# Attention's output products: sixteen to a step in place of up to eighteen

## The chip, the cores and the metric

The kernel runs on one core of a Trainium2 chip. The metric is the device time of one launch in microseconds (us); less is better. Before the change three runs gave 750.22, 750.38 and 750.85 us.

The engines have the names of the profile: PE is TensorE's matmuls and PEld its weight loads, DVE is VectorE, ACT is ScalarE, POOL is GpSimd, and SP issues most of the DMAs.

## The reference

An attention with a feature map for 8 batches of 8 heads, 576 positions and head width 64, and behind it a layer of experts to which each token goes alone.

```python
proj = x @ w_phi                                  # 64 -> 128, for q and for k
proj = proj - max(abs(proj), axis=-1)
phi = concatenate([exp(proj), exp(-proj)])        # 256 features
kv, z = k_phi.T @ v, k_phi.sum(axis=seq)
out = (q_phi @ kv) / (q_phi @ z + 1e-6)           # the attention's output, x of the next part
...
e = argmax(x @ w_gate), or the expert of the token before, by a local gate
out = softmax(x @ w_gate)[e] * (relu(x @ w1[e]) @ w2[e])    # 8 experts, 512 -> 1024 -> 512
```

## The kernel before

**The work.** Attention is done first, then the experts. Two batches and two heads make a unit, and 16 units make the whole. A unit has 1152 tokens, which are 9 chunks of 128; chunk 4 lies half in the one batch and half in the other. Four units (all heads of two batches) make a quarter of the tokens, called bp in the code.

**The steps.** `run` calls `step(p, n)` for p = 0 to 71, two chunks to a step, and goes on with steps without new chunks (the tail) until all is dealt out. TensorE's instructions stay in the order in which they are written; the order of the other engines' instructions is laid out ahead of time by a scheduler and is fixed in the program as well. A step writes, in this order:

- `proj(p)`, L277: the projections of two chunks, k and q, into a PSUM tile pj, of which there are two. VectorE takes the maximum m of it (L280) and subtracts it (sb, L282), ScalarE makes the k features kp out of sb with two exponentials (L286).
- `qtr(p - 1)`, L295: the transposes of the q part of sb from the step before, into the pj tile of that step. ScalarE makes the q features qp from it (L310). In some steps four more transposes follow, those of a finished sum kvs, and ScalarE copies them out (ks, L374). The projections of the step after need this pj tile, so they wait for the last of these reads.
- the chores: some instructions of the gate, the plan and the experts' first weights, which run beside attention.
- sometimes a gate of a sum: a product with the gate's weights into a PSUM tile nm (L383), which ScalarE adds to kvs (L385). Behind it the output products that use the sum are put into the list `todo`.
- the sums over the keys, kvp, of the chunks of step p - 1 (L327, and L340 for chunk 4). When five chunks are in a sum, ScalarE copies it to kvs (L361, L362).
- output products from the head of `todo` (L405), as many as `QUOTA` allows. A chunk has 8 of them, each of which the profile counts as two matmuls. They go in groups of two or three chunks to one nm tile, of which there are two. With the last product of a group its end is written: VectorE adds, takes the reciprocal and multiplies (rc L422 and L423, xo L425), POOL adds the gate's part to lg (L431 to L434), and SP stores xo (L437).

A unit needs five chunks for its first sum and five for the second, so 72 products of one unit come into the list in two portions, 32 and 40, and with two chunks to a step 4.5 steps go by for a unit. Steps come in five kinds by what they hold beside the projections, the transposes and the sums: the four more transposes (a "ks step"), a gate (a "gate step"), chunk 4 (a "kv4 step"), chunk 4 and a gate, and nothing of it. After nine steps, two units, the pattern repeats. The order on TensorE in any row of nine from p = 5 on is: gate, ks, kv4 and gate, ks, gate, ks, gate, kv4, ks.

**The gate of a quarter.** When the last product of the fourth, eighth and twelfth unit has been dealt out, an entry of the list (`ends`, not a product) starts the token gate of that quarter, which the chores then spread over the steps: small VectorE operations on lg (g_mx L567, and more on tiles named g_), four small transposes or products on TensorE (L588, L600, L615, L628 to L633), one exponential on ScalarE (g_ex L648). The last quarter's gate comes in the tail, beside the first experts' work. After the second quarter a plan for the first experts' slots is made in the same way (p_ tiles), their tokens are gathered, and eight of their weight tiles are split by ScalarE (whi, L961) and POOL (wlo, L964).

**The experts** follow the tail: layers 1 and 2 for slots of up to four times 128 tokens, with lines L1084 to L1086 for the matmuls.

Of the kernel before, what the change touches and what calls it, by code (L numbers as in the profile page):

```python
# [33 lines left out]
WE, WR, WL = 8, 3, 2  # L34
FILL = 6
KVLAG = 1
QUOTA = 18

STEP = "step"

# [15 lines left out]
class Kernel:  # L56
# [428 lines left out]
    def step(self, p, n):  # L485
# [24 lines left out]
        for i in pair:  # L510
            if i % NC != 4:
                self.kv(i)
        for _ in range(min(QUOTA, len(self.todo)) if p < n // 2 else len(self.todo)):
            self.todo.pop(0)()
# [840 lines left out]
```

## Time and profile before

| | us |
|---|---|
| median of three runs | 750.38 |
| the profiled execution, whole | 750.71 |
| its span | 748.9 |
| PE busy in it | 725.5 |
| PEld busy | 629.2 |
| DVE busy | 451.6 |
| ACT busy | 340.8 |
| POOL busy | 180.4 |

The span is the stretch from the first to the last instruction that the profile shows; the whole time has 1.81 us more. In the views that follow, times are us from the span's start. A row of a timeline is: start, duration, engine, line, operation, output and inputs, shapes, the number of instructions that the row merges, and in brackets how long the engine was idle before it and which engine's result ended the wait. A row of a table by stretches is: start and end, length, and for each of PE, PEld, DVE, ACT and POOL the busy time with the number of instructions, then the granted clock, the share of the DMA engines and GB/s. In a row of waits stand the total, the number of times and the longest. A busy PE is not PE at its peak: matmuls are pipelined and their ends are modelled.

Attention takes the stretch to about 291 us of the span and the experts the rest.

### The profile page before, as it was taken

To read this page: it belongs to the slowest core of one execution; us is meant where nothing else is said; L and a number is where in the kernel's file an instruction comes from. 1 tells how busy PE (TensorE), PEld (TensorE's weight loads), DVE (VectorE), ACT (ScalarE), POOL (GpSimd) and SP (SyncE) were. 2 spreads that over 40 slices of the span, in tenths; PEclk is the share of its full clock that TensorE was granted. 3 is DMA by queue.
4 is the path that set the end of the run, shared out by engine and by line. 5 is a ranking of instruction groups with operands and counts; after the bars stand their busy time and mean duration, and the time that the engine had idled before them with its cause. 6 is when DMAs were issued, how large, how long until landed. Compare 5 with 4: busy or idle time off the path is not lost. (4 is left out here: it accounts for less than half of the span.)

```text
span 748.9 us, 22153 instructions
## 1 busy us (share of the span) xinstructions
PE 725.5 (97%) x9447; PEld 629.2 (84%) x9447; DVE 451.6 (60%) x828; ACT 340.8 (46%) x644; POOL 180.4 (24%) x306
## 2 busy tenths in 40 slices
PE   6999999999998899999999999999999999999996
PEld 6999989989887888889888975889888778888995
DVE  5888889888878886594536335435522365444413
ACT  5766666666676574323434225332312255241301
POOL 0210103410364674353402041021302102101011
PEclk9999999999999999999999999999999999999999
DMA  7755545554666651064918866334686355434110
GB/s 213 242 169 141 151 129 148 136 157 127 189 191 201 202 176 55 7 198 132 329 63 325 313 237 230 118 127 168 226 291 239 113 221 169 140 127 155 58 39 30
DMA packets 66101, 125.05 MB, mean 167 GB/s; under 512 B 7220, under 2 KB 45300, under 8 KB 65950
## 3 DMA queue, kind: packets, MB, share of 16 engines
q1 hardware_dynamic: 57808, 101.03, 42.1%
q0 software_dynamic: 8016, 22.51, 8.5%
q8 instruction: 75, 1.23, 0.7%
q14 instruction: 26, 0.21, 0.1%
q10 hardware_dynamic: 176, 0.07, 0.0%
HBM read 102.05 MB, written 22.06 MB: 166 GB/s over the span
## 5 line engine op out<-in xcount | busy, mean ns | idle before, releaser
L1129 ACT ACTIVATE hh<-l 128x384 fp32r<-128x384 f32 (+1 forms) x84 | 45.1, 537 | 206.0 <-PE l L1086 206.0
L1084 PE MATMUL l<-xhi,whi 128*128 128x384 f32 (+2 forms) x352 | 124.1, 353 | 0.0
L1086 PE MATMUL l<-xhi,wlo 128*128 128x384 f32 (+2 forms) x352 | 123.6, 351 | 0.0
L1085 PE MATMUL l<-xlo,whi 128*128 128x384 f32 (+2 forms) x352 | 123.3, 350 | 0.0
L1130 DVE SCALAR_TENSOR_TENSOR hl<-l,hh 128x384 fp32r<-128x384 f32 (+1 forms) x84 | 51.6, 615 | 115.9 <-ACT hh L1129 115.8
L1084 PE MATMUL l<-whi,hh 128*128 128x512 f32 x288 | 115.5, 401 | 0.6 <-DVE y L1183 0.6
L964 DVE TENSOR_TENSOR wlo<-wraw,whi 128x1024 fp32r<-128x1024 f32 x80 | 96.5, 1223 | 29.1 <-ACT whi L961 28.9
L1085 PE MATMUL l<-wlo,hh 128*128 128x512 f32 x288 | 113.8, 395 | 0.0
L1086 PE MATMUL l<-whi,hl 128*128 128x512 f32 x288 | 113.7, 395 | 0.0
L286 ACT ACTIVATE kp<-sb 128x512 f32<-128x512 f32 x144 | 83.5, 625 | 59.3 <-DVE sb L282 56.6
L280 DVE TENSOR_REDUCE m<-pj 128x8 f32<-128x1024 f32 x72 | 87.8, 1220 | 35.3 <-PE pj L277 33.3
L961 ACT CAST whi<-wraw 128x1024 fp32r<-128x1024 f32 x88 | 90.4, 1045 | 38.3 <-PE l L1086 14.9
L277 PE MATMUL pj<-first,kq 64*128 64x128 f32 x1152 | 85.2, 289 | 8.3 <-DMA kq<-in_kqT 4.2
L310 ACT ACTIVATE qp<-pj 128x512 f32<-128x512 f32 x144 | 79.7, 595 | 23.5 <-PE pj L295 11.3
L282 DVE TENSOR_TENSOR sb<-pj,m 128x1024 f32<-128x1024 f32 x72 | 88.1, 1223 | 3.5
L405 PE MATMUL nm<-kvs,qp 128*64 128x74 f32 x2304 | 87.2, 228 | 1.9 <-ACT kvs L385 1.0
L277 PEld LDWEIGHTS pj<-first,kq 64*128 64x128 f32 x1152 | 71.5, 191 | 15.4 <-ACT ks L374 5.4
L405 PEld LDWEIGHTS nm<-kvs,qp 128*64 128x64 f32 x2304 | 79.8, 136 | 2.6 <-ACT kvs L385 1.4
L327 PE MATMUL kvp<-v,kp 128*64 128x65 f32 x2048 | 77.7, 225 | 0.8 <-ACT kp L286 0.2
L1186 POOL DMA_INDIRECT out<-y,p_tokm x30 | 34.2, 1141 | 182.4 <-DVE y L1183 165.7
L1084 PEld LDWEIGHTS l<-xhi,whi 128*128 128x128 f32 x352 | 66.2, 188 | 7.2 <-issue 1.6
L327 PEld LDWEIGHTS kvp<-v,kp 128*64 128x64 f32 x2048 | 67.1, 137 | 5.4 <-ACT kp L286 2.0
(224 smaller groups left out, 907.1 us busy)
## 6 DMA issues: line engine op xcount, KB each, us to landing
wraw<-in_w1h SPq DMA_DIRECT2D x44, 512.0 KB, 3.6
wraw<-in_w2h SPq DMA_DIRECT2D x44, 512.0 KB, 5.9
kq<-in_kqT SPq DMA_DIRECT2D x47, 384.0 KB, 4.4
v<-in_va SPq DMA_DIRECT2D x48, 195.0 KB, 3.7
xs<-xo SPq DMA_DIRECT2D x48, 128.0 KB, 2.1
whi<-in_w1h SPq DMA_DIRECT2D x8, 512.0 KB
wlo<-in_w1h SPq DMA_DIRECT2D x8, 512.0 KB, 8.0
whi<-in_w2h SPq DMA_DIRECT2D x8, 512.0 KB
```

The lines of the kernel that those rows point to most:

```text
L277: self.last_pe = self.pe.matmul(t[:, h, i % 2, j, :], kq[r, j, s], self.w2[r], start=True, stop=True)
L280: dve.tensor_reduce(m, f, AX.X, ALU.max, apply_absolute_value=True)
L282: self.last_dve = dve.tensor_sub(sb.rearrange("p h c j f -> p (h c j) f"), f, m.unsqueeze(2).broadcast_to([128, 8, 128]))
L286: self.last_act = act.activation(kp[:, :, :, sg, :].rearrange("p c h f -> p h c f"), sb[:, :, :, 0], AF.Exp, scale=1.0 - 2 * sg)
L310: self.act.activation(qp[:, sg].rearrange("p h (c r k) -> p (h c) r k", c=2, r=2), src, AF.Exp, scale=1.0 - 2 * sg)
L327: self.pe.matmul(t[r, sg, h], kp[:, h, sg, r], v[:, h], start=first and sg + h == 0, stop=last and sg + h == 2)
L405: self.last_num = self.pe.matmul(e["t"][r, c - c0, k], self.ch[i]["qp"][:, sg, h, q0 + r.start:q0 + r.stop], kvs[:, sg, k], start=sg == 0, ...
L961: self.act.copy(hi, raw)
L964: (low or self.dve).tensor_sub(lo[:, c], raw[:, c], hi.bitcast(F32)[:, c])
L1084: mm(o, ah, bh, start=first, stop=False)
L1085: mm(o, ah, bl, start=False, stop=False)
L1086: self.last_pe = mm(o, al, bh, start=False, stop=last)
```

## The change

One constant. `QUOTA` is the most that a step takes from the list of output products, 18 before and 16 now.

```diff
-QUOTA = 18
+QUOTA = 16
```

It is used in the last lines of `step` alone, and not in the tail, where the whole list is dealt out:

```python
for _ in range(min(QUOTA, len(self.todo)) if p < n // 2 else len(self.todo)):
    self.todo.pop(0)()
```

Nothing is added or taken away: the same products are dealt out in the same order, at other places between TensorE's other work, and what depends on a group's last product moves along. Before, nine steps dealt out 18, 14, 18, 18, 18, 18, 18, 18 and 4, which is 144; with the change each deals out 16, 144 as well. The entry that starts a quarter's gate takes a place in the list, so three steps have 15, and from each of them on the list is behind by one more. At p = 72, in the tail, 43 products are left in place of 36.

The first place is on TensorE, in the steps p = 12 to 14, a kv4 step, a ks step and a gate step. The rows are instructions in their order, and the number behind x says how many stand together. Before:

```order
L405 MATMUL nm<-kvs,qp 64x74 x18
L277 MATMUL pj<-first,kq 128x128 x8
L295 MATMUL pj<-first,sb 128x64 x8
L295 MATMUL pj<-first,kvs 128x64 x4
L327 MATMUL kvp<-v,kp 64x65 x16
L405 MATMUL nm<-kvs,qp 64x74 x4
L277 MATMUL pj<-first,kq 128x128 x8
L295 MATMUL pj<-first,sb 128x64 x8
L383 MATMUL nm<-wgi,ks 64x18 x4
L327 MATMUL kvp<-v,kp 64x65 x16
L405 MATMUL nm<-kvs,qp 64x74 x18
```

And now:

```order
L405 MATMUL nm<-kvs,qp 64x74 x16
L277 MATMUL pj<-first,kq 128x128 x8
L295 MATMUL pj<-first,sb 128x64 x8
L295 MATMUL pj<-first,kvs 128x64 x4
L327 MATMUL kvp<-v,kp 64x65 x16
L405 MATMUL nm<-kvs,qp 64x74 x16
L277 MATMUL pj<-first,kq 128x128 x8
L295 MATMUL pj<-first,sb 128x64 x8
L383 MATMUL nm<-wgi,ks 64x18 x4
L327 MATMUL kvp<-v,kp 64x65 x16
L405 MATMUL nm<-kvs,qp 64x74 x16
```

The ks step in the middle had 4 products and has 16; its neighbours have two fewer each.

The second place is on VectorE, where the first quarter's gate begins: the m and sb in these rows are those of p = 23, g_ are the gate's tiles, and the xo ahead is that of the quarter's last group. Before:

```order
L425 TENSOR_TENSOR xo<-nm,rc 128x296
L567 TENSOR_REDUCE g_mx<-lg 128x9
L577 SCALAR_TENSOR_TENSOR g_rs<-lg,consts 128x9
L570 TENSOR_TENSOR g_eq<-lg,g_mx 128x72
L280 TENSOR_REDUCE m<-pj 128x8
L572 TENSOR_TENSOR g_eq<-g_eq,consts 128x72
L282 TENSOR_TENSOR sb<-pj,m 128x1024
L574 TENSOR_REDUCE g_fr<-g_eq 128x9
L646 TENSOR_TENSOR g_ls<-lg,g_mx 128x72
L580 TENSOR_TENSOR g_code<-consts,g_fr 128x9
L581 TENSOR_TENSOR g_code<-g_code,g_rs 128x9
L422 TENSOR_SCALAR rc<-nm 128x4
```

And now:

```order
L425 TENSOR_TENSOR xo<-nm,rc 128x296
L567 TENSOR_REDUCE g_mx<-lg 128x9
L577 SCALAR_TENSOR_TENSOR g_rs<-lg,consts 128x9
L570 TENSOR_TENSOR g_eq<-lg,g_mx 128x72
L646 TENSOR_TENSOR g_ls<-lg,g_mx 128x72
L572 TENSOR_TENSOR g_eq<-g_eq,consts 128x72
L280 TENSOR_REDUCE m<-pj 128x8
L574 TENSOR_REDUCE g_fr<-g_eq 128x9
L282 TENSOR_TENSOR sb<-pj,m 128x1024
L580 TENSOR_TENSOR g_code<-consts,g_fr 128x9
L651 TENSOR_REDUCE g_su<-g_ex 128x9
L581 TENSOR_TENSOR g_code<-g_code,g_rs 128x9
```

Five of the gate's operations stand ahead of the m where three stood, and no rc and xo stand between the m of p = 23 and that of p = 24; before, those of a group of the next unit stood there. For the second and the third quarter the gate's first operations stand one step later than before, in p = 41 in place of 40 and in p = 59 in place of 58, and seven and nine of them are ahead of the m that follows.

## The prediction

> **What bounds the kernel now.** I read the page first, then a table by stretches of the span, cut at the starts of nine-step patterns (units in pairs) and at the experts:
>
> ```profile
> span 748.9 us, 22153 instructions
> ...
> 53.12:86.50 33.38, 33.28 (x873) 31.63 (x873) 29.10 (x55) 23.13 (x52) 3.64 (x16) 1.00 0.53 146
> 86.50:122.61 36.11, 35.12 (x887) 32.25 (x887) 31.72 (x75) 22.90 (x53) 2.91 (x13) 1.00 0.47 134
> 122.61:155.93 33.32, 33.22 (x873) 31.57 (x873) 27.93 (x43) 23.24 (x52) 14.05 (x33) 1.00 0.54 148
> 155.93:192.04 36.11, 35.18 (x886) 32.25 (x886) 31.72 (x75) 22.89 (x53) 3.04 (x14) 1.00 0.48 135
> 192.04:228.86 36.82, 34.28 (x874) 31.79 (x874) 30.12 (x62) 25.88 (x55) 20.57 (x43) 1.00 0.67 206
> 228.86:269.16 40.30, 35.74 (x888) 32.71 (x888) 33.46 (x77) 26.65 (x57) 22.32 (x43) 1.00 0.62 192
> ...
> 300.00:741.00 441.00, 440.37 (x2384) 364.75 (x2382) 205.68 (x341) 145.33 (x210) 87.82 (x81) 1.00 0.49 171
> ```
>
> The experts' stretch is TensorE's without a break: 440.37 of 441 us. So what attention gains or loses moves the end by as much. In attention the six rows hold the same 72 steps' kind of work, 144 products each, and yet take from 33.3 to 40.3 us. The first and third row are clean. The second, fourth and sixth hold a quarter's gate, the fifth the plan and the first weight tiles. Weight loads take 31.6 us of a clean nine and 32.7 of the worst, so the excess is waiting, mostly. Who TensorE's queue waits for, from p = 5 to 67, its three largest rows:
>
> ```profile
> PEld pj L277 <- ACT ks L374: 5.2, 13, 1.2
> PEld pj L295 <- DVE sb L282: 3.6, 7, 1.0
> PEld kvp L340 <- ACT kp L286: 2.1, 8, 0.3
> ```
>
> None of it is for products. TensorE waits for what VectorE and ScalarE make of the projections; the products are filler in which these two catch up. The change deals the filler out evenly.
>
> **The steady pattern.** The starts of TensorE's steps, each the row of its projections, p = 6 to 10 and p = 13 to 15:
>
> ```profile
> 23.98 1.16 PE L277 MATMUL pj<-first,kq 64*128 64x128 f32 x16
> 27.42 1.16 PE L277 MATMUL pj<-first,kq 64*128 64x128 f32 x16
> 31.39 1.16 PE L277 MATMUL pj<-first,kq 64*128 64x128 f32 x16
> 35.09 1.16 PE L277 MATMUL pj<-first,kq 64*128 64x128 f32 x16
> 38.90 1.16 PE L277 MATMUL pj<-first,kq 64*128 64x128 f32 x16
> ...
> 50.14 1.16 PE L277 MATMUL pj<-first,kq 64*128 64x128 f32 x16
> 53.12 1.16 PE L277 MATMUL pj<-first,kq 64*128 64x128 f32 x16
> 57.08 1.16 PE L277 MATMUL pj<-first,kq 64*128 64x128 f32 x16
> ```
>
> Differences of neighbours give lengths: a ks step 3.44 us with 14 products and 3.70 with 18, so a product costs 0.26/4 = 0.065 us. A gate step of 18 takes 3.81, one with chunk 4 as well 3.97. The ks step with 4 products should take 3.70 - 14 x 0.065 = 2.79 and takes 2.98, and the gate step behind it 3.96 in place of 3.81. The rows at the end of another such step, p = 22, show why:
>
> ```profile
> 85.97 0.43 PE L405 MATMUL nm<-kvs,qp 128*64 128x74 f32 x8
> 86.06 0.38 ACT L374 COPY ks<-pj 128x256 f32<-128x256 f32 x1
> 86.50 0.97 PEld L277 LDWEIGHTS pj<-first,kq 64*128 64x128 f32 x16 [0.25 <-ACT ks L374]
> ```
>
> The products are through and the next projections wait for ScalarE's ks, which frees their tile. Then sb and kp come late for the step behind. With 16 products the ks step lasts 3.70 - 0.13 = 3.57, and ks is ready 0.6 us before it is wanted. Per nine steps: seven steps lose 2 products (-0.91), one gains 2 (+0.13), the short one goes from 2.98 to 3.57 (+0.59), and the step behind loses its delay (-0.15): -0.34. There are seven short steps (p = 13, 22, ..., 67): **-2.4 us**. Every group's end (rc, xo) still comes once a step; 7 products more in the tail cost 0.45 and are those that steps p = 23 to 71 didn't do, so they cancel.
>
> The Trainium skill (Perfetto Trace Analysis, Identifying the Most-Contended Engine) says that TensorE's headroom is to be judged by its weight loads and not by its matmul rows. In the first clean row the matmuls leave 0.10 us free and the loads 1.75; by the former seven such nines could gain 0.7 us at most, by the latter 12, and my 2.4 lies between.
>
> **The gates of the first two quarters.** The chain at p = 23:
>
> ```profile
> 87.14 0.15 DVE L422 TENSOR_SCALAR rc<-nm 128x4 f32<-128x4 f32 x1
> 87.25 1.15 ACT L286 ACTIVATE kp<-sb 128x512 f32<-128x512 f32 x2 [0.81 <-DVE sb L282]
> 87.49 0.41 PE L295 MATMUL pj<-first,sb 64*128 64x64 f32 x8
> 87.59 0.47 DVE L425 TENSOR_TENSOR xo<-nm,rc 128x296 f32<-128x296 f32 x1
> 88.44 0.22 POOL L434 TENSOR_TENSOR lg<-lg,xo 128x18 f32<-128x18 f32 x1
> 88.70 0.23 DVE L567 TENSOR_REDUCE g_mx<-lg 128x9 f32<-128x72 f32 x1 [0.64 <-POOL lg L434]
> 89.11 1.22 DVE L280 TENSOR_REDUCE m<-pj 128x8 f32<-128x1024 f32 x1
> 90.43 1.23 DVE L282 TENSOR_TENSOR sb<-pj,m 128x1024 f32<-128x1024 f32 x1
> 90.47 1.16 PE L277 MATMUL pj<-first,kq 64*128 64x128 f32 x16
> 94.64 1.16 PE L277 MATMUL pj<-first,kq 64*128 64x128 f32 x16
> 99.69 1.16 PE L277 MATMUL pj<-first,kq 64*128 64x128 f32 x16
> ```
>
> m stands in VectorE's queue behind g_mx, which waits for POOL, which waited for xo. So it starts 2.61 us after its step's start (86.50), where the projections are there after 1.2. The delay reaches TensorE one step later (4.17 for a 14-product ks step of 3.44), and since rc, xo and eight small operations stand ahead of the next m, once more: 5.05 for 3.97. Lost: 0.73 + 1.08 = 1.81, and as much at the second quarter, whose row above has the same 36.11.
>
> With the change, from a step's start at 0 and these rows' distances. First quarter: the last group ends with p = 22, xo is done at 1.0, POOL at 1.55, five small operations take it to 2.3: m is 1.1 late, sb is done at 4.9. The transposes want it at 3.62 + 1.0 and are 0.3 late, the sums want kp, 0.6 later. No xo stands ahead of the next m, so the delay isn't handed on. But the 15 products of p = 23 follow their gate at once and ScalarE has g_ex, which now comes earlier, ahead of what they wait for: I take 0.75 in all. Second quarter: m of p = 41 is ahead of the gate, that of p = 42 starts at 6.2 where 4.8 would do; sb is done at 8.7, wanted at 8.2, and with kp 0.95 is lost, once. **-1.06 and -0.86, together -1.9.**
>
> **What is given back.** Between a gate's start and its end four steps hold its products, and there ScalarE's exponentials wait for VectorE's small operations, not TensorE for its work. Two products fewer don't shorten such a step; the first sum took 0.13 off each. Bounds: nothing, and 4 x 0.13 = 0.52 a gate. I take the upper one, as the rows of waits name ScalarE: 3 x 0.5 = **+1.5**.
>
> **The plan and the third gate.** Steps p = 52, and p = 60 to 62:
>
> ```profile
> 199.48 1.16 PE L277 MATMUL pj<-first,kq 64*128 64x128 f32 x16
> 204.84 1.16 PE L277 MATMUL pj<-first,kq 64*128 64x128 f32 x16
> ...
> 232.67 1.16 PE L277 MATMUL pj<-first,kq 64*128 64x128 f32 x16
> 237.48 1.16 PE L277 MATMUL pj<-first,kq 64*128 64x128 f32 x16 [0.51 <-ACT ks L374]
> 243.01 1.16 PE L277 MATMUL pj<-first,kq 64*128 64x128 f32 x16
> 249.25 1.16 PE L277 MATMUL pj<-first,kq 64*128 64x128 f32 x16 [1.03 <-ACT ks L374]
> ```
>
> Step p = 52 loses 5.36 - 3.97 = 1.39 to the plan's block of small operations ahead of m. The block moves one step on, behind it comes a longer step (3.84 for 3.44), which hides 0.4 of it: bounds 0 and -1.0, I take **-0.5**. The third gate loses 4.81 - 3.44 and 5.53 - 3.97, 2.93 in all. After, as the second quarter's, 0.95, and 0.35 more for two more small operations ahead of m: -1.6. Against it step p = 62 (6.24), where the list's tokens and the gate's code meet, becomes a gate step, in which ScalarE's order puts qp behind the next kp: +0.5. Together **-1.1**; bounds 0 and -2.
>
> **The sum.** -2.4 - 1.9 + 1.5 - 0.5 - 1.1 = -4.4 us: a span of 744.5, and 746.3 for the profiled execution of 750.71. The three runs' median is 0.33 lower, so I put **746.0** against 750.38.
>
> **The rivals.**
>
> *The waits only move* (17%). They belong to the gate and the plan, not to the products, so each is found again a step later. For it: the gate's chain through POOL is the same. Against it: what stands behind that chain has changed. Then only the short steps' -2.4 and the +1.5 are left: 749.5, no change.
>
> *The gaps close* (15%). With even steps the small delays of clean steps vanish as well. Best lengths with 16: four ks steps of 3.57, three gate steps of 3.68, 3.84 and 3.60 make 32.76 a nine, 0.25 under what I counted, seven times; and nothing is given back: 742.7.
>
> *VectorE has no free step* (13%). The place is p = 24 to 29 and the same steps of the other two gates. Before, two steps there (p = 25 and 29) had no xo, and VectorE caught up; with the change each of the six has one. m to sb takes 1.32, sb to rc 1.15, rc to the end of xo 0.92: 3.4 us, and five small operations of up to 0.2 make 4.4. It decides if this exceeds the step, 3.7 to 3.9: 0.45 a step in three steps is 1.35 a gate and 4.0 in all, in the place of the +1.5. With the short steps' -2.4 and no other gain that is +1.6, **752.0**. Against it: VectorE's 31.72 of 36.11 leaves over 4 us a nine.
>
> That the change deals otherwise than it says is ruled out by the order, but for three steps of 15.
>
> **Chances and range.** The forecast has 55% (744 to 748.5). A measurement can tell about 0.2%, 1.5 us, from no change. Faster: the forecast, the closed gaps and a little of the moved waits, 0.73; within 0.2%: 0.15; slower: 0.12. The range, 742.9 to 750.6, takes in the unknown costs' bounds and the moved waits, and leaves out the free-step rival and half of the closed gaps.
>
> **What would show it.** Right: every ks step at 3.57 and none near 2.98; no wait of L277 for ks in clean nines, which take 33.0; the nines with the first two gates at 35.2 and 35.4, that of the third near 39.4; the experts' stretch as before, shifted. Wrong: xo ending later than the next step's projections step after step, or nines with gates at 36 or more.

## The result, and the profile after

The changed kernel took 747.65 us in the median, beside 751.57 for the kernel before in the same comparison; the ratio is 0.9944, with a 95% interval of 0.9933 to 0.9955. Two later comparisons, on two chips, gave 0.9925 (0.9906 to 0.9944) and 0.9910 (0.9895 to 0.9925). One run of the change (992.03 us, mean granted clock 0.667) and one of the kernel with QUOTA = 32 further down (794.51 us, 0.885) stand apart and are in none of the ratios. It is faster by 4 to 7 us; 746.0 was forecast against 750.38, a ratio of 0.9942.

The profiled execution took 747.42 us. Its span, from the page:

```profile
span 745.6 us, 22169 instructions
```

The stretches, cut at the same steps as before (p = 14, 23, 32, 41, 50, 59 and 68, and 441 us of the experts):

```profile
53.91:86.96 33.05, 33.05 (x877) 31.49 (x873) 29.38 (x55) 23.31 (x52) 3.67 (x16) 1.00 0.54 149
86.96:121.91 34.95, 34.12 (x887) 32.08 (x884) 31.02 (x71) 23.02 (x53) 2.26 (x10) 1.00 0.50 142
121.91:154.80 32.89, 32.87 (x876) 31.35 (x873) 28.04 (x44) 23.39 (x52) 14.01 (x34) 1.00 0.54 149
154.80:190.48 35.68, 34.70 (x888) 32.23 (x885) 31.70 (x74) 23.05 (x53) 3.06 (x13) 1.00 0.48 137
190.48:225.03 34.55, 33.63 (x876) 31.57 (x873) 29.77 (x63) 24.86 (x54) 19.37 (x42) 1.00 0.67 201
225.03:265.08 40.05, 35.68 (x890) 32.75 (x886) 33.65 (x76) 27.26 (x58) 21.55 (x42) 1.00 0.67 203
...
296.00:737.00 441.00, 439.89 (x2382) 364.35 (x2381) 205.49 (x341) 145.29 (x210) 89.51 (x82) 1.00 0.49 171
```

A row of nine steps is called a nine from here on. Every nine is shorter than before. The fifth row, with the plan, lost 2.3 us, the second, with the first gate, 1.2, and the sixth, with the third gate, a quarter. In the experts PE is busy throughout, as before. TensorE's queue, over the same steps, waits much less for ks, sb and kp, and in the second place stands a wait that was not among its largest:

```profile
PEld pj L277 <- ACT ks L374: 2.6, 7, 0.5
PEld nm L405 <- ACT kvs L385: 1.5, 3, 0.7
PEld pj L295 <- DVE sb L282: 1.3, 3, 0.7
```

The steps p = 12 to 14, each row the start of a step's projections:

```profile
46.73 1.16 PE L277 MATMUL pj<-first,kq 64*128 64x128 f32 x16
50.34 1.16 PE L277 MATMUL pj<-first,kq 64*128 64x128 f32 x16
53.91 1.16 PE L277 MATMUL pj<-first,kq 64*128 64x128 f32 x16
57.59 1.16 PE L277 MATMUL pj<-first,kq 64*128 64x128 f32 x16
```

The ks step p = 13 takes 3.57 where it took 2.98, the gate step behind it 3.68 where it took 3.96. The chain of the first gate, from p = 23 on:

```profile
86.96 1.16 PE L277 MATMUL pj<-first,kq 64*128 64x128 f32 x16
89.32 0.26 ACT L648 ACTIVATE g_ex<-g_ls 128x72 f32<-128x72 f32 x1 [1.06 <-DVE g_ls L646]
89.35 1.22 DVE L280 TENSOR_REDUCE m<-pj 128x8 f32<-128x1024 f32 x1
90.21 1.24 PE L405 MATMUL nm<-kvs,qp 128*64 128x74 f32 x30 [0.53 <-ACT kvs L385]
91.38 1.16 PE L277 MATMUL pj<-first,kq 64*128 64x128 f32 x16
92.59 1.23 DVE L280 TENSOR_REDUCE m<-pj 128x8 f32<-128x1024 f32 x1
95.01 1.16 PE L277 MATMUL pj<-first,kq 64*128 64x128 f32 x16
98.85 1.16 PE L277 MATMUL pj<-first,kq 64*128 64x128 f32 x16
```

p = 23 to 25 take 4.42, 3.63 and 3.84, where they took 3.97, 4.17 and 5.05. The delay is taken once, by the products of p = 23, which wait for kvs behind g_ex. The m of p = 24 starts 1.21 after its step's start. Before, it started 3.16 after it (90.47):

```profile
93.63 1.16 DVE L280 TENSOR_REDUCE m<-pj 128x8 f32<-128x1024 f32 x1
```

The third gate has kept two long steps. In p = 61, which takes 5.87, the cause lies one step earlier, in p = 60, which starts at 229.09: its m stands behind the gate's first nine operations on VectorE, g_mx among them, which waits 1.17 for POOL's lg. So it starts 3.04 after its step:

```profile
232.13 1.22 DVE L280 TENSOR_REDUCE m<-pj 128x8 f32<-128x1024 f32 x1
```

The other is p = 63, with waits as large as those of p = 62 before:

```profile
242.48 1.16 PE L277 MATMUL pj<-first,kq 64*128 64x128 f32 x16
243.76 1.23 DVE L280 TENSOR_REDUCE m<-pj 128x8 f32<-128x1024 f32 x1 [0.21 <-PE pj L277]
243.81 0.38 PE L754 MATMUL pj<-first,lr 6*128 6x6 f32 x2
244.97 0.15 DVE L757 COPY p_probe<-pj 128x6 f32<-128x6 f32 x1
245.18 0.28 PE L588 MATMUL pj<-first,g_code 128*9 128x128 f32 x1 [0.98 <-DVE p_probe L757]
...
248.81 1.16 PE L277 MATMUL pj<-first,kq 64*128 64x128 f32 x16 [1.01 <-ACT qp L310]
```

The list's tokens are transposed (L754), their copies stand behind m on VectorE, and the gate's next operation on TensorE waits for the copies; the step takes 6.33, where p = 62 took 6.24.

### The profile page after: what moved, and what is told of

Same layout as the page of the kernel before. It is cut to its first block, busy times and chain, and to the rows that moved or that the text cites. A ratio compares the mean times of both kernels' runs of the same rounds, so it can differ in the third digit from the quotient of the medians.

```text
span 745.6 us, 22169 instructions
## 1 busy us (share of the span) xinstructions
PE 724.3 (97%) x9447; PEld 630.2 (85%) x9447; DVE 451.9 (61%) x828; ACT 341.3 (46%) x644; POOL 182.8 (25%) x305
## 3 DMA queue, kind: packets, MB, share of 16 engines
q8 instruction: 75, 1.23, 0.7%
## 5 line engine op out<-in xcount | busy, mean ns | idle before, releaser
L277 PE MATMUL pj<-first,kq 64*128 64x128 f32 x1152 | 85.8, 290 | 7.5 <-DMA kq<-in_kqT 4.2
L277 PEld LDWEIGHTS pj<-first,kq 64*128 64x128 f32 x1152 | 72.0, 192 | 14.2 <-issue 4.2
L1086 PEld LDWEIGHTS l<-xhi,wlo 128*128 128x128 f32 x352 | 66.2, 188 | 5.5
```

Of the source, the lines that this page charges most:

```text
L277: self.last_pe = self.pe.matmul(t[:, h, i % 2, j, :], kq[r, j, s], self.w2[r], start=True, stop=True)
L1086: self.last_pe = mm(o, al, bh, start=False, stop=last)
```

## The experiments

There were twelve runs, four to a call, those of one call on the same chip; three of them repeat the kernel before or the change. This table of the nines' lengths (us, by the starts of L277) is read with all of them; the last column runs from p = 5 to p = 68.

| first step | 5 | 14 | 23 | 32 | 41 | 50 | 59 | sum |
|---|---|---|---|---|---|---|---|---|
| what is in it | | | gate 1 | | gate 2 | plan | gate 3 | |
| before | 33.17 | 33.38 | 36.11 | 33.32 | 36.11 | 36.82 | 40.30 | 249.21 |
| before, third call | 33.17 | 33.23 | 36.12 | 33.64 | 36.12 | 36.59 | 42.31 | 251.18 |
| the change | 33.03 | 33.05 | 34.95 | 32.89 | 35.68 | 34.55 | 40.05 | 244.20 |
| the change, first call | 33.02 | 33.03 | 34.95 | 32.88 | 35.43 | 34.38 | 40.02 | 243.71 |
| the change, third call | 33.03 | 33.09 | 34.95 | 32.94 | 35.44 | 35.78 | 39.93 | 245.16 |
| short step split | 33.08 | 33.40 | 35.34 | 33.17 | 35.23 | 36.08 | 38.91 | 245.21 |
| QUOTA = 17 | 33.49 | 33.57 | 35.50 | 33.31 | 35.87 | 34.94 | 39.43 | 246.11 |
| gates a step later | 32.95 | 33.17 | 36.15 | 33.11 | 36.28 | 36.61 | 40.46 | 248.73 |
| order alone | 33.69 | 33.17 | 35.40 | 33.53 | 36.72 | 35.88 | 38.97 | 247.36 |
| order alone, third call | 33.18 | 33.50 | 35.41 | 33.58 | 36.74 | 34.84 | 39.49 | 246.74 |
| 16, gates not later | 32.80 | 32.79 | 35.24 | 33.20 | 36.00 | 34.98 | 39.28 | 244.29 |
| QUOTA = 32 | 35.06 | 36.31 | 38.72 | 37.20 | 38.89 | 38.57 | 42.26 | 267.01 |
| 16, tokens a step later | 32.99 | 32.79 | 34.95 | 32.91 | 35.43 | 36.54 | 41.61 | 247.22 |
| 16 and the order | 33.03 | 32.83 | 35.08 | 32.81 | 35.55 | 35.49 | 37.98 | 242.77 |

The first two gates' nines repeat within 0.3 us from execution to execution. The nine with the plan doesn't, for the change 34.4 to 35.8, nor does the third gate's in the kernel before, 40.3 and 42.3. What follows p = 68 takes between 479.0 and 485.0 us of the span in these profiles, for the change alone 479.9 to 483.3. So differences between the whole times of two profiles can't be put down to the edits; the nines and the medians of several runs can.

**The change again**, the code of the change.

> The change once more, beside the three kernels that follow, so that all four stand against the same runs of before. By the first comparison of it, 4.2 us under before (ratio 0.9944).

Measured: 745.88 us against 751.82, ratio 0.9925.

**The short step alone.**

```diff
+        quota = 10 if p % 9 == 3 else QUOTA        # QUOTA stays 18
-        for _ in range(min(QUOTA, len(self.todo)) if p < n // 2 else len(self.todo)):
+        for _ in range(min(quota, len(self.todo)) if p < n // 2 else len(self.todo)):
```

> QUOTA stays at 18, only the step ahead of each short one gives up 8 of its products to it: of nine steps the last two deal 10 and 12 in place of 18 and 4, all others and the steps in which the gates begin stay as before. My theory (products are cover, and the short step has too few of them) gives the short ks step 3.70 - 6 x 0.065 = 3.31 in place of 2.98, the kv4 step ahead of it 8 x 0.065 = 0.52 less, the step behind 0.15 less: -0.34 a nine, seven times, 2.4 us under before (ratio 0.9968), with the gates' nines losing their 1.8 as before. The rival that the gain of the change is all in where the gates begin gives no change (ratio 1.000). The rival that every step must have 16 (the closed gaps) gives less than 1 us.

Measured: 0.9950 (0.9936 to 0.9964), 3.8 us. Neither the sum nor the rival holds. The clean nines gained 0.1 instead of 0.34, and the gates' nines, which were to stay, became shorter by 0.8, 0.9 and 1.4 us. First, why the clean ones gained so little. The starts of p = 12 to 14, and below them the m of p = 12 and 13 on VectorE:

```profile
46.29 1.16 PE L277 MATMUL pj<-first,kq 64*128 64x128 f32 x16
49.52 1.16 PE L277 MATMUL pj<-first,kq 64*128 64x128 f32 x16
52.91 1.16 PE L277 MATMUL pj<-first,kq 64*128 64x128 f32 x16
```

```profile
47.50 1.23 DVE L280 TENSOR_REDUCE m<-pj 128x8 f32<-128x1024 f32 x1 [0.69 <-PE pj L277]
51.10 1.21 DVE L280 TENSOR_REDUCE m<-pj 128x8 f32<-128x1024 f32 x1
```

The two steps take 3.23 and 3.39, together 6.62 where 3.73 + 2.98 = 6.71 stood. VectorE's work from one m to the next takes 3.60 there (m, sb, two small operations on a table, a group's rc and xo), more than either step: the second m starts 1.58 after its step, the first 1.21. The ks step was to take 3.31 and takes 3.39, and p = 14 behind it takes 3.90 where 3.81 was to come. By these rows, what the short step gains in cover its neighbour lacks.

**QUOTA = 17.**

```diff
-QUOTA = 18
+QUOTA = 17
```

> QUOTA = 17: nine steps deal 17, 15, six times 17, and 10, and the gates of the quarters begin in the same steps as with 18. My theory: seven steps with a product less, -0.46, one with one more, +0.07, the short one 3.70 - 8 x 0.065 = 3.18 in place of 2.98, +0.20, the one behind -0.15: -0.34 a nine again, 2.4 us under before; of that up to 0.8 is given back in the gates' steps that are bound by ScalarE: -1.6 to -2.4 (ratio 0.9968 to 0.9979). That the gates' place is the whole: no change. That only the fully even deal helps: less than 1 us.

Measured: 0.9950 (0.9933 to 0.9967). The clean nines got longer, by 0.32 and 0.19 in the first two, where 0.34 was to be gained; what was gained lies in the gates' nines (0.61, 0.24 and 0.87) and in the plan's (1.88). Why a product less in each step gained nothing, the starts of p = 10 to 12 and the weight loads of p = 10's products show:

```profile
39.04 1.16 PE L277 MATMUL pj<-first,kq 64*128 64x128 f32 x16
42.74 1.16 PE L277 MATMUL pj<-first,kq 64*128 64x128 f32 x16
46.54 1.16 PE L277 MATMUL pj<-first,kq 64*128 64x128 f32 x16
```

```profile
41.42 1.23 PEld L405 LDWEIGHTS nm<-kvs,qp 128*64 128x64 f32 x34
```

The ks step with 17 takes 3.70 and the gate step 3.80: as long as with 18. The rows of the same step before, with 18, and in the change, with 16:

```profile
41.29 1.23 PEld L405 LDWEIGHTS nm<-kvs,qp 128*64 128x64 f32 x36
...
41.87 1.10 PEld L405 LDWEIGHTS nm<-kvs,qp 128*64 128x64 f32 x32
```

17 and 18 products take 1.23, 16 take 1.10. Likewise p = 6 takes 3.57 with 15 and with 16. Products cost 0.13 a pair, and an odd one as much as a pair: neighbours in the list go to the two halves of the output's partitions. The Trainium skill (TensorEngine Tiling (Array Packing), Key Properties) says that different tiles of the array can load and multiply in parallel; the trace agrees, the 17th and 18th product go in the time of one.

**The gates a step later.**

```diff
         lt = self.lg.pop(bp)
         if not self.tail:
+            yield STEP
             yield STEP
         L = lt[:, :, 0:E]
```

> QUOTA stays at 18, the gates of the first three quarters wait one step more before their first operation, nothing else is changed. In the first gate's chain g_mx then finds lg long done: the 0.64 of waiting and the chain over xo and POOL go, and five small operations of together 0.9 stay ahead of the m of p = 24. My theory: two thirds of the 1.8 us that each of three gates loses, with the later place of the plan: 2 to 3 us under before (ratio 0.996 to 0.9973), about as much as the gates' terms of the sum without what is given back. The rival that the waits only move: no change (within 0.5 us). The rival of the free step: slower, since p = 24's own xo and the gate's operations meet, by up to 1 us a gate.

Measured: 0.9967 (0.9957 to 0.9977), 2.5 us, as my theory had it, but not by its way. The edit writes all of a gate's operations a step later. Those on TensorE moved (L588 of the first gate from p = 26 to p = 27); VectorE's first ones the scheduler laid out where they had been, among p = 23's:

```profile
89.58 0.23 DVE L568 TENSOR_REDUCE g_mx<-lg 128x9 f32<-128x72 f32 x1 [0.64 <-POOL lg L434]
```

g_mx waits its 0.64 as before, p = 24 and 25 take 4.18 and 5.06 as before, and the nines of the first two gates lose nothing. What moved is the plan: p = 51 and 52 take 7.91 where they took 8.80. In the profiled execution the nines lose 0.5 and what follows them up to the experts 0.9, and the start gives 1.3 back, where the granted clock was 0.57 over p = 2 (3.96 for 2.58). As a test of the gates' place it failed.

**The order alone.** In the change, with 17 and with the split step, all with 10 products or more in p = 22, the gate's g_ls stands ahead of the m of p = 23 on VectorE; in the kernel before it stands behind sb. So this kernel deals as before and only writes g_ls and g_ex earlier.

```diff
         dve.tensor_tensor(eq, L, bc(mx, E), ALU.is_ge)
+        ls = sm([128, NC, E], "ls")
+        with self.soon():
+            dve.tensor_sub(ls, L, bc(mx, E))
+        ex = sm([128, NC, E], "ex")
+        with self.soon():
+            act.activation(ex, ls, AF.Exp)
         yield
...
-        ls = sm([128, NC, E], "ls")
-        dve.tensor_sub(ls, L, bc(mx, E))
-        ex = sm([128, NC, E], "ex")
-        act.activation(ex, ls, AF.Exp)
-        yield
```

> QUOTA stays at 18 and every step deals what it dealt before. Only the gate's subtraction g_ls and its exponential g_ex are written right behind g_eq, and ahead of what isn't the gate's, so that on VectorE and ScalarE the gate's operations stand as they do with 17 and with the split short step: g_ls ahead of the m of p = 23, g_ex ahead of p = 23's qp, and between the m of p = 23 and that of p = 24 three fewer of the gate's operations. Theory of the order (formed from the first four runs: with 17, and with 12 products in the short step, the gates' nines shrank by 0.2 to 0.9 though no gate began later, since the delay is then taken once, at the products of p = 23, and not handed on to p = 25): p = 23 takes about 4.9, p = 24 3.5 and p = 25 4.2, the three gates' nines lose 0.6 to 1.4 each, and the whole is 2 to 3 us under before (ratio 0.996 to 0.9973). My first theory (the products must stand in the short step, and the list must be a step later): the gates' nines stay within 0.2, no change (ratio 1.000).

> The kernel with the old deal and the other order of the gate once more: it came out at 0.9906, lower than the change in either comparison, though on another chip. Theory of the order: it reaches at least half of the change's gain without moving a product, 0.990 to 0.997. If its first result belonged to that chip: 1.000.

Measured: 0.9906 (0.9889 to 0.9923), and in the third call 0.9917 (0.9902 to 0.9933), beside 0.9910 for the change. Without moving a product it reaches the change's time. The steps p = 23 to 25 of the third call, and VectorE's rows among them:

```profile
86.50 1.16 PE L277 MATMUL pj<-first,kq 64*128 64x128 f32 x16
90.12 1.38 PE L405 MATMUL nm<-kvs,qp 128*64 128x74 f32 x36 [0.74 <-ACT kvs L385]
91.43 1.16 PE L277 MATMUL pj<-first,kq 64*128 64x128 f32 x16
94.87 1.16 PE L277 MATMUL pj<-first,kq 64*128 64x128 f32 x16
98.99 1.16 PE L277 MATMUL pj<-first,kq 64*128 64x128 f32 x16
```

```profile
88.97 0.23 DVE L573 TENSOR_TENSOR g_ls<-lg,g_mx 128x72 f32<-128x72 f32 x1
89.12 1.22 DVE L280 TENSOR_REDUCE m<-pj 128x8 f32<-128x1024 f32 x1
92.88 1.21 DVE L280 TENSOR_REDUCE m<-pj 128x8 f32<-128x1024 f32 x1
```

4.93, 3.44 and 4.12: 12.49 where 13.19 stood. A group's rc and xo still stand ahead of the m of p = 24, which starts 1.45 after its step and not 3.16. The theory of the order holds for gates 1 and 3 (-0.7 and -0.8 to -1.3 against the first profile); the nine of gate 2 is 0.6 longer. The edit also takes a yield out of the gate, and the plan behind it now reaches p = 49 (3.94 in place of 2.97), where ScalarE's qp waits 1.32 for the plan's p_ue. So it isn't the whole: by the traces it is worth 1.9 to 2.5 us up to p = 68 against the first profile of before, and 4.4 against that of the third call, where the change has 6.0. That the medians are level (750.66 us beside 750.31) comes from elsewhere: behind p = 68 the third call's profile of the order takes 480.7 us, the change's 483.3 and that of before 484.8. No run shows whether this comes from the edit or from chance.

**Sixteen, with the gates in their old steps.**

```diff
-QUOTA = 18
+QUOTA = 16
...
-                self.todo.append(lambda: self.ends(u // NHP))
+                end = self.todo.pop()
+                self.todo.append(lambda: (end(), self.ends(u // NHP)))
```

> QUOTA = 16, but the entry that starts a gate takes no place of its own in the list: no step has 15, the list isn't put behind, and the gates begin in p = 22, 40 and 58 as with 18, one step earlier than in the change. My term for the gates rests on their place: without it the second gate's nine loses its 0.86 again and the third its 1.6, less 0.5: slower than the change by about 2 us (ratio 0.997 to before). Theory of the order: the even deal alone gives the good order, so the first and second gates' nines are near 35.3 and the third's, without the meeting of the list's tokens and the gate's code behind a gate step, near 39.2: as fast as the change or up to 1.5 us faster (ratio 0.991 to 0.994).

Measured: 0.9936 (0.9922 to 0.9950); a direct comparison with the change on that chip wasn't made. The profiled execution met two falls of the granted clock to 0.50, at 11 to 15 and 328 to 333 us, outside the nines. A clean nine and the first gate's:

```profile
54.04:86.83 32.79, 32.79 (x875) 31.32 (x872) 29.38 (x55) 23.32 (x52) 3.66 (x16) 1.00 0.53 148
86.83:122.07 35.24, 34.29 (x890) 32.18 (x887) 31.43 (x75) 23.03 (x53) 3.14 (x14) 1.00 0.50 138
```

The seven nines sum to 244.29, the change's to 244.20. Beginning a step later, the change gains 0.3 at each of the first two gates and gives 0.8 back at the third: nothing in all. My first theory is out.

**The opposite dose.**

```diff
-QUOTA = 18
+QUOTA = 32
```

> The opposite dose: QUOTA = 32 deals 32, 0, 32, 8, 32, 0, 32, 8, 0 in nine steps, the same 144 products. If the products are cover: a step of 32 takes 3.81 + 14 x 0.065 = 4.72, a ks step of none can't be shorter than the 2.98 of the step with 4 in before, which VectorE's and ScalarE's work sets; four of the former, three of the latter, two with 8 (3.05 and 3.08) and the delays behind make 34.1 to 35 a nine in place of 33.3: 5 to 12 us slower than before (ratio 1.007 to 1.016). If only the gates' order and place counted: within 2 us of before.

Measured: 1.0212 (1.0197 to 1.0228), 16 us slower, above the range given; the nines say the same, +17.8 us in their sum. Two falls of the granted clock are in that sum (0.79 and 0.86 over 90 to 95 and 95 to 100 us, 0.66 over 245 to 250); by one minus the clock, times the stretch, they are worth about 3.4 us, an estimate. The first nine has none:

```profile
19.90:54.96 35.06, 33.92 (x872) 31.73 (x873) 28.69 (x47) 22.78 (x52) 7.05 (x22) 1.00 0.66 203
```

The weight loads hardly changed (31.73, before 31.38): the same products cost the same, and most of the rest is waiting. That products are cover, and that clumps of them are lost cover, holds.

**The tokens a step later**, with QUOTA = 16:

```diff
-WAIT, HOLD = 3, 2
+WAIT, HOLD = 4, 2
```

> The change with one number more: the list's tokens are transposed one step later (WAIT 4 in place of 3), so that they don't fall into the step of the third gate's code, where the step p = 63 takes 6.33 us with 0.98 of waiting for p_probe. If that meeting is the cause, p = 63 falls to about 4, another step gets 0.3 to 0.8 more, and the whole is 1 to 2 us under the change (ratio 0.990 to 0.992 to before). If the wait belongs to the tokens' gather alone (they come late whatever stands beside), the next step gets it: as the change.

Measured: 0.9958 (0.9944 to 0.9971), slower than the change was in the other calls. p = 63 fell to 4.14, and p = 64 took 7.57:

```profile
251.04 0.20 PE L600 MATMUL pj<-g_dg,consts 9*9 9x9 f32 x2 [1.18 <-DVE p_probe L757]
255.59 1.65 PE L277 MATMUL pj<-first,kq 64*128 64x128 f32 x16 [1.95 <-ACT ks L374]
```

The copies stand behind m in this step too, and the gate's next operation on TensorE, now another, waits for them. Meeting the code (L588) wasn't the cause.

**Before, the change, the order and both, on one chip.**

> The kernel before once more, with a profile of its own beside the three that follow. The same code: ratio 1.000. It shows which of the steps that the change seemed to shorten are long in every execution and which only in the first profile: the gates' steps (p = 24 and 25: 4.17 and 5.05; p = 52: 5.36; p = 61 and 62) should be the same within 0.1, while those with an idle time that is put down to issue (p = 53 with 4.73, p = 56 with 4.54) may not. If p = 53 and 56 come out near 3.8, up to 1.8 us of the fifth nine's gain of 2.3 isn't the change's.

> The change a third time, beside its rivals on the same chip: 0.993 to 0.995 of before.

> The change and the order together. The even deal gives the first gate's order by itself already, so nothing is gained there; the clean nines gain their 0.3 (2 us in seven), and in the second and third gates g_ls stands a place or two earlier and the m of p = 59 ahead of the gate's block. If the two gains are of different places: 1 to 2 us under the better of the two (0.988 to 0.992). If they are one and the same: as the change (0.993 to 0.995).

The first three are kernels told of above. The last joins the change to the edit of the order:

```diff
-QUOTA = 18
+QUOTA = 16
...
+        with self.soon():
+            dve.tensor_sub(ls, L, bc(mx, E))
```

Measured: before 0.9999 (757.81 us), the change 0.9910, both together 0.9876 (0.9858 to 0.9893; 748.13 us beside 750.31 for the change). It is the fastest of all, by 0.3% against the change. Its nine with the third gate takes 37.98, where the change has 39.93: p = 61 to 63 take 3.84, 4.07 and 5.35 in place of 5.86, 3.57 and 6.34. In the first two gates nothing is added, as expected: the change has the order there already. In the second profile of before the first two gates' steps repeat (p = 24, 25 and 43: 4.19, 5.05, 5.05). Two others that were expected to repeat don't: p = 52, with the plan, took 5.57 in place of 5.36, and p = 61, in the third gate, 6.93 in place of 5.53. Of the steps with unexplained idle time p = 53 took 3.95 in place of 4.73 and p = 57 4.61 in place of 3.73. So the change's gain in the fifth nine, 2.27 by the first pair of profiles, is 0.81 by this one, and that in the nine with the third gate, 0.25 by the first pair, is 2.38.

## Why the prediction was right, point by point

The number came out (0.9942 forecast, 0.9944 measured), and the mechanism at its centre: the products are cover for VectorE and ScalarE. That the two ratios agree so closely is luck: three of the five terms were off and made up for each other, and the later comparisons gave 0.9925 and 0.9910. By nines, forecast and measured, by the first pair of profiles and by the third call's:

| nine | forecast | first pair | third call |
|---|---|---|---|
| three clean ones, each | -0.34 | -0.14, -0.33, -0.43 | -0.14, -0.14, -0.70 |
| gate 1 | -0.34 - 1.06 + 0.5 = -0.90 | -1.16 | -1.17 |
| gate 2 | -0.34 - 0.86 + 0.5 = -0.70 | -0.43 | -0.68 |
| plan | -0.34 - 0.5 = -0.84 | -2.27 | -0.81 |
| gate 3 | -0.34 - 1.1 + 0.5 = -0.94 | -0.25 | -2.38 |
| sum | -4.4 | -5.01 | -6.02 |

The seven products more in the tail came as said: from the start of p = 71 to the experts' first matmul 14.06 became 14.52. From -5.01 to the 3.3 us between the spans it is 0.9 at the start, ahead of p = 5, where the code is the same and the second profile of before has it too, 0.25 between p = 68 and the experts, and 0.5 in the experts.

**The short steps (-2.4): right.** The clean nines' mean, -0.30, makes -2.1 in seven. Ahead of the plan the ks steps outside the gates are at 3.57 or 3.58, as written, but for p = 17 with 3.78. The 0.10 us of a clean nine in which PE wasn't busy set no bound: PE's busy time itself fell, in the first clean row from 33.28 to 33.05. The price of a product, 0.065, was wrong: it is 0.13 a pair, and an odd one costs as much. As 18, 16, 14 and 4 are all even, the sum didn't notice.

**The gates of the first two quarters (-1.9): the size right for the first, the reason wrong.** p = 23 was to take 4.37 and takes 4.42. But the step of the argument that "no xo stands ahead of the next m, so the delay isn't handed on" fails. In the kernels with 17, with the split step and with the order alone an xo stands there, and the delay is hardly handed on either (p = 25 takes 4.05, 4.18 and 4.12, a step of its kind with 18 products 3.97); and with 16 but no gate later, the nines sum to the same. What the longer ks step of p = 22 brings is another order of the gate's small operations on VectorE and ScalarE, and that alone gives the first gate 0.7 of its 1.16. The prediction had seen that g_ex comes earlier, and booked it as a cost. The second gate was over-sized a little: p = 43 still takes 4.89, its chain loses 1.25 in place of 0.95.

**What is given back (+1.5): too much.** The four steps that hold the first gate's products took 16.21 (p = 26 to 29) and take 15.91 (p = 27 to 30); I had them stay. It is 0.2 there, and 0.2 to 0.5 at the second gate.

**The plan (-0.5): under-sized.** p = 51 and 52 together fell from 8.80 to 7.77, in the third call from 9.02 to 7.84, which is at the lower of my two bounds or below it. Of the rest of that nine's 2.27 some is the products' share, and p = 53, 56 and 57 have idle times that differ between executions of the same code.

**The third gate (-1.1): the mechanism failed.** The chain that was to lose 1.3 in place of 2.93 loses 2.4 in p = 60 and 61 (3.95 and 5.87, where 3.57 and 3.85 are clean): nine small operations, the first of which waits 1.17 for POOL, stand ahead of one m. p = 63 takes 6.33: the copies behind m weren't in my account of that stall, only its neighbourhood. The 2.38 of the third call doesn't speak for the term: 1.4 of it is the granted clock in p = 61 before (last section).

**The rivals.** "The waits only move" is out for the first gate: p = 24 and 25 are short and no later step has their loss. At the third gate it is what the first pair of profiles shows. "VectorE has no free step" is out: with an xo in each of p = 24 to 29 these steps take 3.58 to 4.07. "The gaps close" was near: with no gate later, clean nines of 32.80 and 32.79 were reached, where 32.76 was the best.

## What to carry to other kernels

Filler work between two engines' turns is worth most when each turn has the same share of it; what a short turn gets must not make its neighbour short. When a change moves work on one engine, look at how the order on the others was laid out anew, and try that order by itself: here it gave about as much as the change in the medians, and both together the most. A forecast may hold for another reason than its own, and only a kernel with the one and without the other tells.

## What the runs showed of the hardware that was not expected

**The order of small operations sets what they cost.** Between the sb of p = 23 and the m of p = 24 VectorE has ten small operations in the kernel before and ten in that with the order alone, nine of them the same. In the former the three g_su come last; the first starts 0.49 behind xo, when g_ex is done, the others 0.26 and 0.21 behind their forerunners, whose results they use, and the ten take 2.06 us from the first's start to that of m. In the latter g_ex is early, the g_su are mixed with rc, g_fr and g_code, all ten start 0.04 to 0.14 after each other, and they take 1.30.

**TensorE's clock falls after short idle times, in some executions.** The second profile of before, p = 61, whose projections and transposes had waited:

```profile
238.56 1.16 PE L277 MATMUL pj<-first,kq 64*128 64x128 f32 x16 [0.51 <-ACT ks L374]
240.50 0.46 PE L295 MATMUL pj<-first,sb 64*128 64x64 f32 x8 [0.78 <-DVE sb L282]
```

and the granted clock (third number from the end) in the stretches that follow, and behind a wait of 2.46 us in the experts:

```profile
240.56:243.50 2.94, 2.74 (x62) 2.31 (x64) 2.83 (x6) 2.23 (x5) 0.22 (x1) 0.65 0.79 229
...
334.00:336.00 2.00, 1.90 (x5) 1.52 (x6) 2.00 (x7) 0.89 (x1) 1.04 (x1) 0.50 0.75 272
```

The step took 6.93. By stretches of 1 us from 241 to 245 the clock was 0.71, 0.50, 0.50 and 0.58, which comes to about 3.4 us at half. In the first profile the same waits of 0.51 and 0.78 left the clock at 1.00 and the step took 5.53: 1.4 us by chance. The Trainium skill (TensorE: Matmul & The Clock Gate, What's actually happening) says that the clock is set by how busy TensorE was in windows of about 3.4 us that run freely, so that chance decides where a gap falls; the trace agrees with that. By the table in that section of the Trainium skill the clock falls after at least one idle window of that length. Here idle times of 0.51 and 0.78 us were enough. The kernel with the tokens later met such a fall too (the 1.65 in place of 1.16 in its last row above, at a clock of 0.72).

The mean clock of each run says how often it happens. The first profile of before, with a mean of 0.998, has no fall until behind 746 us; the second, with 0.993, has the two above. On its chip 25 of the 29 runs of before have means of 0.993 to 0.996, and none of the 16 runs of the change, the order and both is below 0.997. So there before mostly met falls that these three didn't. At the 1.4 us of p = 61 a fall, one or two of them would be 1.4 to 2.8 of the 7.2 us that the change gained there, an estimate. That they come less often because the change idles less is likely and not shown: with 16 and the gates not later, the means on another chip are 0.994 to 0.998.
